# Mamba-2 scan and low-rank mixer: one more block of batch 0 in split one-pass products, and all pieces in another order

## The chip, the cores and the metric

The kernel runs on one core of a Trainium2 chip. The metric is the device time of one execution in microseconds. Before the change it is 234.9 us, the median of three runs (232.25, 234.90, 235.66).

## What is computed

Two blocks follow one another. The first is a Mamba-2 scan over 4 batches, 8 heads, 768 steps, head dimension 32 and state size 16, in chunks:

```python
for c in range(nc):
    cum = np.cumsum(la, axis=-1)
    L = np.exp(cum[..., :, None] - cum[..., None, :]) * causal
    y_intra = ((Cc @ Bc.T) * L) @ xc
    y_inter = (Cc @ state) * np.exp(cum)[..., None]
    y[:, :, sl] = y_intra + y_inter
    state = decay_full * state + (Bx * decay_from_j).sum(axis=2)
```

Its output, regrouped to `x` of shape (4, 768, 256), goes through a mixer, all in fp32:

```python
h = x.transpose(0, 2, 1) @ U @ V          # rank 32, over the sequence
u = x + h.transpose(0, 2, 1)
out = u + np.maximum(u @ w_ch1, 0.0) @ w_ch2     # 256 -> 1024 -> 256
```

The inputs U, V, w_ch1 and w_ch2 arrive as fp64 words and are turned into fp32 on the chip.

## The kernel before

The order of all work is written out by hand, in five strings, `PLANS` (lines 31 to 68). PLANS[0] is the order of the loads on SP's queue; PLANS[1] to [4] are the orders of the pieces. `follow` (line 909) reads a plan word by word and issues the instructions of each; each engine executes its own in that order. Words with a scan letter act on pair k = 3 x (batch) + the word's number, where a pair is 256 steps of the sequence; plan b works on batch b, so `m-1` in plan 1 is pair 2, in batch 0. Words with a mixer letter carry a lag: `U1.0.3` in plan 1 is batch 1 - 1 = 0, block 0, row group 3. A block is 384 tokens, half a sequence.

Scan letters, each with its engine:

| word | what | engine |
|---|---|---|
| P, Q | B and C times decay factors (`prep`, line 436) | VectorE |
| D, E | B times decay to the end (`decayed`, 448) | VectorE; GpSimd in batch 0 |
| T, V | transposes of those (`turning`, 460) | TensorE, then ScalarE, in part VectorE |
| g | products C B (`gram`, 495), into four PSUM banks x, x, z, z | TensorE |
| m, M | causal mask of the x banks, of the z banks (`mask`, 510) | VectorE |
| s, u | chunk states; their decayed sum (`state`, 529, `update`, 545) | TensorE; VectorE |
| i, j, n | the output's parts from the state and from within the chunk (`inter`, `intra`) | TensorE; j may need a small VectorE copy `settled` |
| y, t, O | copy out of PSUM, transpose to token order | ScalarE; TensorE |

The whole program's letters: `A`, `k`, `K` make the decay factors; `c` converts a piece of weights from fp64 words to fp32 in three parts with two ScalarE operations among five VectorE operations (`to_fp32`, 379; c0 is U and V, c1 to c5 are w_ch1, c6 to c9 w_ch2); `R` splits a quarter of a weight in two parts (`refine`, 416; R0 to R3 for w_ch1, R4 to R7 for w_ch2); `v` spreads V; `F n` puts n idle 128-column products into the next PSUM bank (`fill` and `idle`, 130 to 150).

Mixer letters (`mixer`, 692): `p` and `x` are the low-rank products with U and V, `a` adds them to u. Then each block's two large products are made in one of two ways.

- *Plain*, in batch 0 only: `U` (`plain`, 761) makes one 128-row group of relu(u @ w_ch1) in fp32, two products of 128x128 by 128x384; `d` (`down`, 795) makes the second product in four pieces of four products each and then two pieces of transposes and the output copy. It reads the fp32 weights `w1f` and `w2f`.
- *Split*, everywhere else: every fp32 number is written as a near half of 12 bits and a far half; a product is then three products in the type fp32r (near x near, far x both, and so on)[...]. `S` (`split`, 740) splits u: one ScalarE and two VectorE operations. `f` (`first`, 772) makes four of the six products of a row group and has ScalarE rescale the sum, `e` (`second`, 778) the other two and the near half of the relu, `h` (`third`, 786) takes the far half on VectorE and, at every second row group, a third tile that joins both (`joined`, 735). `d` is then twelve pieces of four one-pass products and two of transposes.

The products go to the PSUM tags x and z, two banks each, alternately; x, z are shared with `g` and `x`. Tiles of the tag `words` (15 buffers of 4 KB per partition) hold raw weight words, conversion temporaries, the relu's plain output (four tiles for a block) or its three halves (twelve tiles for a block). The tile for the split u takes the place of `w1f`, so S needs R0 to R3 and all U of w1f to be done.

Of the kernel before, what the change touches and what calls it, by code (L numbers as in the profile page):

```python
# [10 lines left out]
FP32 = mybir.dt.float32  # L11
INT32 = mybir.dt.int32
UINT32 = mybir.dt.uint32
FP32R = mybir.dt.float32r
WCOLS = 512
NWORDS = 15


NEAR = 1.0 - 2.0 ** -13
# [2 lines left out]
ALU = mybir.AluOpType  # L22
# [7 lines left out]

PLANS = {
    0: (
        'V0 B0 X0 B1 X1 B2 X2 B3 U0 w0 w1 X3 w2 B4 X4 w3 w4 w5 B5 w6 X5 w7 B6 w8 X6 '),
    1: (
        'A0 A1 Q-3.0 Q-3.2 Q-3.1 k0 V-3.0.0 V-3.1.1 Q-2.0 K0 F2 g-3 Q-2.2 m-3 M-3 Q-2.1 V-2.0.2 '
        'D-3 F1 s-3 D-2 V-2.1.2 n-3 u-3 Q-1.0 g-2 Q-1.2 i-3 V-1.0.2 m-2 Q-1.1 M-2 F1 V-1.1.3 '
        'E-1.0 F2 s-2 j-3 y-3 g-1 u-2 n-2 E-1.1 i-2 s-1 m-1 j-2 u-1 y-2 M-1 F2 O-3.0 P0 n-1 c0 '
        'i-1 c0 j-1 c0 y-1 t-2 T0 O-1.1 c2 c1 D0 v0 c2 c1 p1 c1 T0 x1 s0 a1.0 c2 a1.1 c3 U1.0.0 '
        'U1.0.1 u0 c3 U1.1.0 D1 U1.1.1 P1 T1 c3 g0 i0 m0 M0 T1 c4 c4 U1.0.2 U1.0.3 s1 c5 c4 c6 c5 '
        'R1 F1 U1.1.2 U1.1.3 u1 n0 L4 g1 P2 D2 j0 T2 T2 c6 m1 U1.0.4 M1 c5 U1.0.5 y0 U1.1.4 c8 '  # L40
        'U1.1.5 c7 i1 c6 c8 c7 R4 n1 g2 P3 j1 s2 m2 u2 y1 L5 R2 M2 R0 U1.0.6 t0 U1.0.7 c7 T3 R3 '
        'T3 U1.1.6 D3 U1.1.7 n2 i2 g3 c9 P4 c8 D4 T4 t1 R6 m3 c9 M3 c9 R2 P5 R1 T4 d1.0 d1.0 d1.0 '
        'R4 j2 s3 R3 D5 y2 u3 d1.0 R7 d1.0 L6 t2 R6 g4 p0 d1.0 m4 M4 R5 R7 n3 '),
    2: (
        'x1 s1 a1.0 d2.1 L4 R0 R5 S1.0 d2.1 D3 d2.1 a1.1 f1.0.0 f1.0.1 u1 T2 T2 P3 e1.0.0 d2.1 '
        'f1.0.2 e1.0.1 f1.0.3 e1.0.2 f1.0.4 e1.0.3 f1.0.5 h1.0.0 h1.0.1 h1.0.2 e1.0.4 h1.0.3 '
        'f1.0.6 e1.0.5 i0 h1.0.4 f1.0.7 e1.0.6 d2.1 e1.0.7 j0 h1.0.5 h1.0.6 d2.1 h1.0.7 y0 T3 T3 '
        'g2 m2 i1 n1 s2 M2 d1.0 d1.0 S1.1 u2 f1.1.0 f1.1.1 d1.0 d1.0 e1.1.0 s3 D4 e1.1.1 P4 '
        'h1.1.0 d1.0 f1.1.2 d1.0 f1.1.3 e1.1.2 h1.1.1 d1.0 d1.0 h1.1.2 j1 d1.0 e1.1.3 y1 u3 '
        'h1.1.3 f1.1.4 t0 d1.0 d1.0 f1.1.5 e1.1.4 d1.0 e1.1.5 L5 f1.1.6 h1.1.4 h1.1.5 f1.1.7 t1 '  # L50
        'e1.1.6 T4 e1.1.7 h1.1.6 h1.1.7 n2 i2 d1.0 g3 T4 d1.0 j2 d1.1 d1.1 d1.1 d1.1 m3 y2 d1.1 '
        'd1.1 M3 P5 d1.1 d1.1 d1.1 d1.1 d1.1 t2 d1.1 p0 D5 g4 d1.1 m4 M4 d1.1 '),
    3: (
        'x1 a1.0 n0 i0 s1 a1.1 j0 S1.0 y0 f1.0.0 f1.0.1 f1.0.2 e1.0.0 e1.0.1 T2 u1 f1.0.3 e1.0.2 '
        'h1.0.0 f1.0.4 h1.0.1 e1.0.3 T2 h1.0.2 h1.0.3 t0 f1.0.5 e1.0.4 f1.0.6 e1.0.5 f1.0.7 '
        'h1.0.4 e1.0.6 i1 e1.0.7 n1 s2 g2 h1.0.5 h1.0.6 j1 h1.0.7 d1.0 m2 d1.0 d1.0 M2 S1.1 y1 '
        'f1.1.0 f1.1.1 d1.0 e1.1.0 e1.1.1 h1.1.0 d1.0 d1.0 f1.1.2 f1.1.3 h1.1.1 u2 d1.0 e1.1.2 '
        'e1.1.3 d1.0 h1.1.2 i2 h1.1.3 d1.0 d1.0 f1.1.4 f1.1.5 n2 e1.1.4 e1.1.5 j2 f1.1.6 h1.1.4 '
        'h1.1.5 y2 f1.1.7 t1 e1.1.6 t2 h1.1.6 e1.1.7 p0 h1.1.7 d1.0 d1.0 '),
    4: (  # L60
        'x1 a1.0 d2.0 d2.0 a1.1 d2.1 d2.1 S1.0 d2.1 d2.1 f1.0.0 d2.1 d2.1 f1.0.1 e1.0.0 d2.1 '
        'e1.0.1 h1.0.0 d2.1 f1.0.2 d2.1 h1.0.1 f1.0.3 d2.1 d2.1 d2.1 e1.0.2 f1.0.4 e1.0.3 f1.0.5 '
        'h1.0.2 f1.0.6 h1.0.3 e1.0.4 h1.0.4 e1.0.5 f1.0.7 d2.1 e1.0.6 h1.0.5 h1.0.6 d2.1 e1.0.7 '
        'h1.0.7 d1.0 S1.1 d1.0 d1.0 d1.0 d1.0 d1.0 d1.0 f1.1.0 f1.1.1 d1.0 e1.1.0 d1.0 e1.1.1 '
        'h1.1.0 d1.0 f1.1.2 h1.1.1 d1.0 d1.0 f1.1.3 e1.1.2 f1.1.4 h1.1.2 e1.1.3 d1.0 f1.1.5 '
        'f1.1.6 e1.1.4 h1.1.3 f1.1.7 e1.1.5 h1.1.4 e1.1.6 h1.1.5 h1.1.6 d1.0 e1.1.7 h1.1.7 d1.1 '
        'd1.1 d1.1 d1.1 d1.1 d1.1 d1.1 d1.1 d1.1 d1.1 d1.1 d1.1 d1.1 d1.1 '),
}


# [1 line left out]
def kernel(  # L72
# [27 lines left out]
    nc = tc.nc  # L100
    P = 128
    NB, NH, S, D = x.shape
# [3 lines left out]
    DM = NH * D  # L106
# [3 lines left out]
    NCB = DM // P  # L110
    HS = S // 2
    W = DF // 4
    NBL = S // HS
    NQ = NM // 2
    Q = 32
# [23 lines left out]
    def bank(tag, *dims):  # L139
        t = psum.tile([P, *dims], FP32, tag=tag, name=tag, bufs=BANKS[tag])  # L140
        if fills[0]:
            idle(t if len(dims) == 1 else t.rearrange(
                {2: "p a b -> p (a b)", 3: "p a b c -> p (a b c)"}[len(dims)]), fills[0])
        fills[0] = 0
        return t

    def fill(n):
# [10 lines left out]
        out=a_sb,  # L158
        in_=a.rearrange("(g b) h (c s) -> g (b h c) s", g=2, s=P).rearrange(
            "g r s -> r g s"))  # L160
# [36 lines left out]
    w1 = [const.tile([P, NCB, DF], FP32R, name=f"w1{i}") for i in range(3)]  # L197
    w1all = mix.tile([P, NQ, NCB, W], FP32, tag="u", name="w1f", bufs=1)
    w1f = [w1all[:, c] for c in range(NQ)]
    w2 = [const.tile([P, NM, DM], FP32R, name=f"w2{i}") for i in range(3)]  # L200
# [56 lines left out]
    ident = const.tile([P, P], FP32)  # L257
# [28 lines left out]
    for v in range(2):  # L286
        half = slice(v * H, v * H + H)
        nc.vector.tensor_tensor(out=ref[half, half], in0=upto[half, half],
                                in1=low[v][half, half], op=ALU.subtract)
# [22 lines left out]
    for b in range(NB):  # L312
        g, o = divmod(b * NH * NC, R)
        nc.vector.tensor_scalar(
            out=la[:, b].rearrange("p c h -> p h c"),
            in0=la_ps[:, g, o:o + NH * NC].rearrange("p (h c) -> p h c", h=NH),
# [10 lines left out]
    for v in range(2):  # L327
        half = slice(v * H, v * H + H)
# [363 lines left out]
    def mixer(b):  # L692
# [34 lines left out]
        def block(n, k):  # L727
            return uT[:, n, ts(k, HS)]
# [19 lines left out]
        def products(t, pairs, start):  # L748
            for lhsT, rhs in pairs:
                nc.tensor.matmul(out=t, lhsT=lhsT, rhs=rhs, start=start, stop=True,  # L750
                                 skip_group_check=True)
                start = False

        def scaled(t):
            nc.scalar.activation(t, t, AF.Copy, scale=1.0 + EPS)  # L755
# [30 lines left out]
        def third(j, m):  # L786
# [5 lines left out]
            if m % 2:  # L792
                joined(near, far, both)

        def down(j):

            def terms(n, which, half):
                return [(w2[v][:, m, ts(n, P)], gs[j, m // 2][v][:, m % 2])
                        for v in which for m in range(NQ * half, NQ * half + NQ)]

            def whole(n, t):
                u = block(n, j)
                nc.vector.tensor_tensor(out=u, in0=t, in1=u, op=ALU.add)  # L803

            ts_ = [bank("xz"[n], HS) for n in range(NCB)] if b else None
            if b:
                for v in range(2):
                    for n in range(NCB):
                        for half in range(2):
                            products(ts_[n], terms(n, (v,), half), v + half == 0)  # L810
                            if v and half:
                                scaled(ts_[n])
                            yield
            for n in range(NCB):
                t = ts_[n] if b else bank("xz"[n], HS)
                for half in range(2):
                    if b:
                        products(t, terms(n, (2,), half), False)
                    else:
                        products(t, [(w2f[m // 2][:, m % 2, ts(n, P)], gT[j, m // 2][:, m % 2])  # L820
                                     for m in range(NQ * half, NQ * half + NQ)], half == 0)
                    if half:
                        whole(n, t)
                    yield
            o = (mix.tile([P, 2 * WCOLS], FP32, tag="o", name="o") if b else raw.tile(
                [P, 2 * WCOLS], FP32, tag="words", name="words", bufs=NWORDS))
            o = o[:, :HS // P * DM].rearrange("p (k n d) -> p k n d", k=HS // P, n=NCB)
            for n in range(NCB):
                t = bank("w", HS // P, P)
                for k in range(HS // P):  # L830
                    nc.tensor.transpose(out=t[:, k], in_=block(n, j)[:, ts(k, P)], identity=ident)  # L831
                nc.scalar.copy(out=o[:, :, n], in_=t)
                if n:
                    nc.sync.dma_start(
                        out=out[b].rearrange("(j k p) m -> j p k m", j=NBL, p=P)[j],
                        in_=o.rearrange("p k n d -> p k (n d)"))
                yield

        us, gs, gT = {}, {}, {}
        downs = {}  # L840

        def piece(j):
            next(downs.setdefault(j, down(j)))

        return SimpleNamespace(p=project, x=mixed, a=added, S=split, f=first, e=second, h=third,
                               d=piece, U=plain)
# [50 lines left out]
    def ytokens_of(k, v):  # L897
# [9 lines left out]
                 v=lambda n: spread())  # L907
# [49 lines left out]
```

## Time and profile before

The profiled execution took 233.18 us, of which the span of the profile is 231.5; the median of the runs is 234.9. TensorE's granted clock was 1.00 throughout.

| row of the profile | count | busy us | mean ns |
|---|---|---|---|
| L750 products, one pass (u and words, x and z) | 576 records | 124.1 | 337 to 347 |
| L750 products, plain, up (yT) | 64 records | 23.6 | 496, 487 |
| L750 products, plain, down (words, o) | 64 records | 21.9 | 489 |
| L789 VectorE, far half of the relu (`third`) | 48 | 26.6 | 554 |
| L737 VectorE, joined halves of the relu | 24 | 23.0 | 958 |
| L755 ScalarE, rescaling | 60 | 28.6 | 476 |
| L135 TensorE, fills (all forms) | 18 records | 6.0 | 275 to 928 |

"Busy" of a matmul includes time in which it overlaps its neighbours in the array, so a mean is longer than the distance from one to the next. Where a count of work is wanted, the distance between starts on the timeline is the better measure. A plain product leaves two records, a one-pass product one.

### The profile page before, as it was taken

The numbers are of one execution on the slowest core, as the hardware profiler recorded it, in microseconds if no ns is written. First come the engines' busy times: TensorE is split into PE (matmuls) and PEld (weight loads), VectorE is DVE, ScalarE is ACT, GpSimd is POOL, SyncE is SP. The second block draws the span as 40 slices with busy tenths as digits, with TensorE's granted clock in tenths as the row PEclk, the third lists the DMA queues.
The fourth block names the chain that finished last, engine by engine and source line by source line (L and its number), as shares of the span: only waits on it lengthen the run. The fifth ranks groups of instructions, "written<-read, shape, count | busy, mean of one in ns | idle before, by whom it ended". The sixth has DMA issues, their size and how long they took to land.

```text
span 231.5 us, 6973 instructions
## 1 busy us (share of the span) xinstructions
PE 222.2 (96%) x3010; PEld 183.0 (79%) x3010; DVE 159.6 (69%) x341; ACT 122.3 (53%) x287; POOL 6.7 (3%) x22
## 2 busy tenths in 40 slices
PE   7988899999999999999999999999999999999992
PEld 4857656566665756889999897988988799999991
DVE  3487799988989879399557517898447635836720
ACT  3243665968946651775555413783635334834711
POOL 4041000000000000000000000000000000000000
PEclk9999999999999999999999999999999999999999
DMA  3994779899940080005300102000000010110101
GB/s 77 128 131 75 187 134 282 176 230 143 121 63 4 3 156 3 3 0 109 56 1 3 69 2 70 4 1 6 0 3 0 21 49 0 35 37 0 36 32 68
DMA packets 69202, 14.56 MB, mean 63 GB/s; under 512 B 63476, under 2 KB 67380, under 8 KB 69172
## 3 DMA queue, kind: packets, MB, share of 16 engines
q1 hardware_dynamic: 69172, 14.13, 31.0%
q8 instruction: 23, 0.38, 0.7%
q14 instruction: 7, 0.06, 0.1%
HBM read 10.98 MB, written 3.15 MB: 61 GB/s over the span
## 4 chain that ended last, share of the span: by engine, by line
PE 94%; DVE 2%; issue 1%; ACT 1%; POOL 0%; POOLq 0%; ACTq 0%
PE x L750 32%; PE z L750 31%; PE y L630 4%; PE y L654 4%; PE x L504 3%; PE w L831 3%; PE w L704 3%; PE w L472 2%; PE w L675 2%; PE w L539 2%; PE x L135 2%; PE x L715 1%; PE z L504 1%; PE z L715 1%; PE x L472 1%
## 5 line engine op out<-in xcount | busy, mean ns | idle before, releaser
L750 PE MATMUL z<-u,w 128*128 128x384 f32 x144 | 33.0, 344 | 0.0
L750 PE MATMUL x<-u,w 128*128 128x384 f32 x144 | 32.9, 347 | 0.0
L755 ACT ACTIVATE x<-x 128x384 f32<-128x384 f32 x30 | 14.3, 476 | 31.0 <-PE x L750 30.4
L750 PE MATMUL x<-words,w 128*128 128x384 f32 x144 | 29.2, 341 | 0.3 <-DVE M L517 0.3
L750 PE MATMUL z<-words,w 128*128 128x384 f32 x144 | 29.0, 337 | 0.0
L750 PEld LDWEIGHTS x<-u,w 128*128 128x128 f32 x144 | 25.1, 188 | 1.1 <-ACT x L755 0.2
L750 PEld LDWEIGHTS x<-words,w 128*128 128x128 f32 x144 | 24.9, 188 | 0.8 <-DVE M L517 0.4
L750 PEld LDWEIGHTS z<-words,w 128*128 128x128 f32 x144 | 25.2, 188 | 0.2 <-issue 0.2
L750 PEld LDWEIGHTS z<-u,w 128*128 128x128 f32 x144 | 24.9, 188 | 0.5
L789 DVE SCALAR_TENSOR_TENSOR words<-x,words 128x384 fp32r<-128x384 f32 x24 | 13.3, 554 | 17.2 <-ACT words L784 17.1
L737 DVE SCALAR_TENSOR_TENSOR words<-words 128x768 fp32r<-128x768 f32 x24 | 23.0, 958 | 1.7 <-PE z L750 0.7
L755 ACT ACTIVATE z<-z 128x384 f32<-128x384 f32 x30 | 14.3, 477 | 10.6 <-PE z L750 10.1
L789 DVE SCALAR_TENSOR_TENSOR words<-z,words 128x384 fp32r<-128x384 f32 x24 | 13.3, 554 | 4.6 <-ACT words L784 4.4
L784 ACT ACTIVATE words<-x 128x384 fp32r<-128x384 f32 x24 | 11.8, 493 | 4.5 <-PE x L750 4.1
L784 ACT ACTIVATE words<-z 128x384 fp32r<-128x384 f32 x24 | 11.9, 494 | 4.0 <-PE z L750 3.9
L630 PE MATMUL y<-T,Sm 32*64 32x64 f32 x352 | 12.8, 239 | 0.5 <-DVE settled L581 0.3
L803 DVE TENSOR_TENSOR yT<-x,yT 128x384 f32<-128x384 f32 x8 | 4.4, 554 | 12.6 <-PE x L750 12.6
L630 PEld LDWEIGHTS y<-T,Sm 32*64 32x64 f32 x352 | 9.6, 131 | 4.1 <-issue 0.7
L559 DVE SCALAR_TENSOR_TENSOR S<-S,kept,w 128x64 f32<-128x64 f32 x40 | 11.2, 280 | 2.1 <-PE w L539 0.5
L750 PE MATMUL x<-yT,w1f 128*128 128x384 f32 x32 | 11.9, 496 | 0.0
L445 DVE TENSOR_TENSOR BC<-bc,F 128x512 f32<-128x512 f32 (+2 forms) x18 | 9.9, 557 | 2.8 <-DMA bc<-in_B_dram 2.6
L750 PE MATMUL z<-yT,w1f 128*128 128x384 f32 x32 | 11.7, 487 | 0.0
(152 smaller groups left out, 386.8 us busy)
## 6 DMA issues: line engine op xcount, KB each, us to landing
words<-in_moe_w_ch_dram SPq DMA_DIRECT2D x7, 512.0 KB, 4.9
x<-in_x_dram SPq DMA_DIRECT2D x24, 128.0 KB, 3.4
out_dram<-o SPq DMA_DIRECT2D x6, 384.0 KB, 2.5
bc<-in_B_dram SPq DMA_DIRECT2D x24, 64.0 KB, 3.6
bc<-in_C_dram SPq DMA_DIRECT2D x12, 128.0 KB, 3.7
out_dram<-words SPq DMA_DIRECT2D x2, 384.0 KB, 3.5
words<-in_moe_w_ch_dram SPq DMA_DIRECT2D x2, 256.0 KB, 3.8
words<-in_moe_V_dram SPq DMA_DIRECT2D x1, 192.0 KB
```

What stands on the lines that cost most here:

```text
L445: nc.vector.tensor_tensor(out=part, in0=bc_sb[k].rearrange("p h i c n -> p (i c) h n")[:, g], in1=F[:, b, q].rearrange("p h i c -> p (i c) ...
L472: nc.tensor.transpose(out=tp[:, i, v], in_=s["BC"][:, i, c + v].rearrange("p h n -> p (h n)"), identity=ident)
L504: nc.tensor.matmul(out=g[r][cols, c], lhsT=s["T"][rows, 0, c, cols], rhs=s["Cm"][rows, :, :, ts(2 * c + p, Q)].rearrange("r v t i -> r v i ...
L559: done = nc.vector.scalar_tensor_tensor(out=new, in0=st["S", b], scalar=kept[:, b, j, None], in1=add, op0=ALU.mult, op1=ALU.add)
L630: product = nc.tensor.matmul(out=y[p][ts(r % 2, H), r // 2, c], lhsT=own[ts(r, Q)], rhs=s["T"][ts(r, Q), 1, :, ts(2 * c + p, Q)].rearrange ...
L654: product = nc.tensor.matmul(out=y[p][ts(i, Q), n, c], lhsT=x_sb[k][half, c, h], rhs=s["M"][half, h // 2, c, h % 2], start=fresh(k, p, [i] ...
L704: nc.tensor.matmul(out=p[ts(q, Q)], lhsT=U_sb[:, c], rhs=ytok[b][:, c, ts(q // 2, P)], start=(c == 0), stop=(c == NC - 1), skip_group_chec ...
L737: nc.vector.scalar_tensor_tensor(out=both, in0=near.bitcast(FP32), scalar=-EPS, in1=far.bitcast(FP32), op0=ALU.mult, op1=ALU.add)
L750: nc.tensor.matmul(out=t, lhsT=lhsT, rhs=rhs, start=start, stop=True, skip_group_check=True)
L755: nc.scalar.activation(t, t, AF.Copy, scale=1.0 + EPS)
L784: nc.scalar.activation(gs[j, m // 2][0][:, m % 2], t, AF.Relu, scale=NEAR)
L789: nc.vector.scalar_tensor_tensor(out=far[:, m % 2], in0=gs["t", j, m], scalar=0.0, in1=near[:, m % 2].bitcast(FP32), op0=ALU.max, op1=ALU. ...
```

## The change

The constant `PLAIN` becomes 1: in batch 0 only block 0 is still made with plain products. Block 1 gets the split form, so its eight `U1.1` words go, and `S1.1`, `f1.1.0` to `7`, `e1.1.0` to `7` and `h1.1.0` to `7` come in plan 1 (the last as `h2.1.7` in plan 2), with fourteen pieces `d2.1` instead of six in plan 2. In all plans the order of the words is another; plan 1 starts its conversions `c` earlier, has 26 fill units where all plans together had 9, and its first mixing word x1 comes after more of batch 1's scan. In the loads, X3 and B4 now stand ahead of w0 to w2, and w5 to w7 ahead of X5, with B5 earlier. The new function `rows` is used only if `b >= ROWS`, with ROWS = 9, so for no batch.

```diff
+PLAIN = 1
+ROWS = 9
...
     0: (
-        'V0 B0 X0 B1 X1 B2 X2 B3 U0 w0 w1 X3 w2 B4 X4 w3 w4 w5 B5 w6 X5 w7 B6 w8 X6 '),
+        'V0 B0 X0 B1 X1 B2 X2 B3 U0 X3 B4 w0 w1 w2 X4 w3 w4 B5 w5 w6 w7 X5 w8 B6 X6 '),
     1: (
-        'A0 A1 Q-3.0 Q-3.2 Q-3.1 k0 V-3.0.0 V-3.1.1 Q-2.0 K0 F2 g-3 Q-2.2 m-3 M-3 Q-2.1 V-2.0.2 '
-        'D-3 F1 s-3 D-2 V-2.1.2 n-3 u-3 Q-1.0 g-2 Q-1.2 i-3 V-1.0.2 m-2 Q-1.1 M-2 F1 V-1.1.3 '
-        'E-1.0 F2 s-2 j-3 y-3 g-1 u-2 n-2 E-1.1 i-2 s-1 m-1 j-2 u-1 y-2 M-1 F2 O-3.0 P0 n-1 c0 '
-        'i-1 c0 j-1 c0 y-1 t-2 T0 O-1.1 c2 c1 D0 v0 c2 c1 p1 c1 T0 x1 s0 a1.0 c2 a1.1 c3 U1.0.0 '
-        'U1.0.1 u0 c3 U1.1.0 D1 U1.1.1 P1 T1 c3 g0 i0 m0 M0 T1 c4 c4 U1.0.2 U1.0.3 s1 c5 c4 c6 c5 '
-        'R1 F1 U1.1.2 U1.1.3 u1 n0 L4 g1 P2 D2 j0 T2 T2 c6 m1 U1.0.4 M1 c5 U1.0.5 y0 U1.1.4 c8 '
-        'U1.1.5 c7 i1 c6 c8 c7 R4 n1 g2 P3 j1 s2 m2 u2 y1 L5 R2 M2 R0 U1.0.6 t0 U1.0.7 c7 T3 R3 '
-        'T3 U1.1.6 D3 U1.1.7 n2 i2 g3 c9 P4 c8 D4 T4 t1 R6 m3 c9 M3 c9 R2 P5 R1 T4 d1.0 d1.0 d1.0 '
-        'R4 j2 s3 R3 D5 y2 u3 d1.0 R7 d1.0 L6 t2 R6 g4 p0 d1.0 m4 M4 R5 R7 n3 '),
+        'K0 D-3 A0 Q-3.0 F5 A1 Q-3.2 Q-3.1 V-3.0.0 V-3.1.1 Q-2.0 Q-2.2 k0 g-3 m-3 M-3 V-2.0.2 F1 '
+        's-3 Q-2.1 V-2.1.2 n-3 D-2 Q-1.0 u-3 s-2 F2 g-2 Q-1.2 u-2 i-3 Q-1.1 E-1.0 E-1.1 m-2 '
+        'V-1.0.2 M-2 V-1.1.3 g-1 j-3 P0 T0 m-1 y-3 M-1 T0 c0 s-1 F2 g0 c0 i-2 D0 c0 u-1 n-2 j-2 '
+        'P1 y-2 T1 T1 m0 c1 M0 F3 s0 D1 c1 u0 c2 c1 c3 i-1 c2 F3 O-3.0 n-1 F2 t-2 j-1 s1 c2 c3 c3 '
+        'y-1 v0 u1 R1 F4 O-1.1 c5 c4 n0 R0 i0 g1 R1 m1 p1 M1 j0 P2 x1 c5 a1.0 y0 a1.1 c6 c6 T2 T2 '
+        'c4 c5 U1.0.0 c6 U1.0.1 L4 D2 U1.0.2 U1.0.3 n1 c4 i1 t0 g2 s2 j1 R4 m2 c7 y1 M2 c8 c8 c7 '
+        'P3 L5 R3 U1.0.4 U1.0.5 u2 c7 F1 U1.0.6 T3 T3 U1.0.7 R5 n2 g3 R3 D3 i2 P4 R2 m3 T4 M3 c8 '
+        'T4 F3 t1 g4 j2 s3 m4 c9 c9 y2 c9 R2 M4 R0 D4 d1.0 d1.0 d1.0 P5 L6 S1.1 R4 R6 d1.0 f1.1.0 '
+        'f1.1.1 R5 f1.1.2 e1.1.0 f1.1.3 e1.1.1 u3 e1.1.2 d1.0 e1.1.3 h1.1.0 h1.1.1 f1.1.4 h1.1.2 '
+        't2 d1.0 f1.1.5 R7 f1.1.6 f1.1.7 h1.1.3 e1.1.4 e1.1.5 R6 h1.1.4 e1.1.6 e1.1.7 h1.1.5 p0 '
+        'T5 T5 h1.1.6 i3 '),
...
-            ts_ = [bank("xz"[n], HS) for n in range(NCB)] if b else None
-            if b:
+            parts = b or j >= PLAIN
+            ts_ = [bank("xz"[n], HS) for n in range(NCB)] if parts else None
+            if parts:
...
-                t = ts_[n] if b else bank("xz"[n], HS)
+                t = ts_[n] if parts else bank("xz"[n], HS)
...
-                    if b:
+                    if parts:
                         products(t, terms(n, (2,), half), False)
```

Plans 2 to 4 are other orders of the same words as before, except for the words of batch 0's block 1 named above; one `n`, `i`, `M` or `h` word here and there stands in the neighbouring plan.

## The prediction

> **What bounds the kernel now.** I read the page's busy shares and slices first, then busy times by stage, then the engines' timelines around the place where the change acts.
>
> ```profile
> span 231.5 us, 6973 instructions
> PE 222.2 (96%) x3010; PEld 183.0 (79%) x3010; DVE 159.6 (69%) x341; ACT 122.3 (53%) x287; POOL 6.7 (3%) x22
> PE   7988899999999999999999999999999999999992
> DVE  3487799988989879399557517898447635836720
> PE 94%; DVE 2%; issue 1%; ACT 1%; POOL 0%; POOLq 0%; ACTq 0%
> ```
>
> TensorE is the chain: 94% of the path. But in slices 5 to 18 (from about 29 us) VectorE is nearly as full as TensorE. The windows, cut at events of the TensorE timeline, say how full:
>
> ```profile
> 4.40:20.00 15.60, 13.79 (x246) 11.33 (x252) 9.57 (x30) 5.68 (x22) 2.53 (x4) 1.00 0.94 131
> 20.00:31.20 11.20, 10.49 (x375) 7.91 (x374) 8.80 (x30) 6.80 (x19) 1.48 (x3) 1.00 0.62 142
> 31.20:65.80 34.60, 34.31 (x579) 22.07 (x580) 31.77 (x77) 25.73 (x58) 0.00 (x0) 1.00 0.91 175
> 65.80:81.40 15.60, 15.60 (x236) 10.02 (x234) 14.18 (x29) 9.43 (x21) 0.00 (x0) 1.00 0.07 12
> 81.40:141.90 60.50, 60.29 (x730) 51.18 (x722) 39.19 (x75) 29.20 (x69) 0.00 (x0) 1.00 0.20 39
> ```
>
> The columns after the length are PE, PEld, DVE, ACT, POOL busy. 31.2 us is where batch 0's mixing product `x1` starts; 65.8 is where its first down product `d1.0` starts (I call this **the mark**); 81.4 ends plan 1. From 4.4 to 65.8 VectorE is busy 9.57 + 8.80 + 31.77 = 50.1 of 61.4 us, so idle 11.3: 6.0 before 20 us, 2.4 up to 31.2, 2.8 after. After 81.4 it is busy 65%, with room. Two lines of timelines show that both engines arrive at the mark together:
>
> ```profile
> 65.01 0.76 DVE L517 TENSOR_TENSOR M<-x,causal 128x256 int32<-128x256 int32 x2 [0.58 <-PE z L504]
> 65.78 5.33 PE L750 MATMUL x<-words,o 128*128 128x384 f32 x16
> ```
>
> The mask `m3` frees the two x banks at 65.7; the down product, which writes an x bank, starts at 65.78. The stretch is balanced: work taken from TensorE there buys nothing unless VectorE comes sooner too.
>
> [...]the eight plain products from 65.78 to 70.94 take 5.16 us, 0.645 each (two records a product), and eight one-pass products take 0.174 each:
>
> ```profile
> 131.48 1.55 PE L750 MATMUL z<-words,w 128*128 128x384 f32 x8
> 132.87 1.55 PE L750 MATMUL x<-words,w 128*128 128x384 f32 x8
> ```
>
> (1.39 us from start to start, over 8). The ratio is 3.7. [...] PE counts 10.49 of 11.2 us busy between 20 and 31.2, yet the pieces there, by start to start, hold less. So I count work by start-to-start times.
>
> **The change part by part.**
>
> *TensorE, products.* 32 plain products go (16 up, 16 down), 96 one-pass products come: 32 x 0.645 = 20.6 us out, 96 x 0.174 = 16.7 in, **-3.9 us**.
>
> *TensorE, fills.* The plans before hold 9 fill units, the new ones 26. A 128-column unit takes 0.27 (two at 19.39, next work at 19.93). Twelve new ones of that size are 3.2; five of 48 columns I put at 0.1 each (unmeasured; 0.05 to 0.27): **+3.7**. TensorE's total is then unchanged within 0.2. Fills lie where TensorE would wait; they cost only if the wait is not there.
>
> *VectorE.* One more split (L732 954 + L737 958 ns), eight `third` (L789, 554 each), four joins (958 each): 1.9 + 4.4 + 3.8 = +10.2; three settle copies of 0.152 go: **+9.7**. *ScalarE:* ten more scalings of 0.476 and a near half of 0.855: **+5.6**, in a queue 53% busy; the split's near half stands on the path to the first one-pass product, but at a point where TensorE still has plain products.
>
> *Behind the mark.* Of the pieces ahead of the mark, the new order takes away the eight `U1.1` (16 plain products, 10.3) and adds g4 (0.63), s3 (0.38), j2 (0.43) and the 17 fill units (3.7): TensorE has 10.3 - 1.4 - 3.7 = 5.2 less ahead. As its total is 0.2 less, **5.0 us more lies behind the mark.** Before, 231.5 - 65.8 = 165.7 us follow it. If that stretch runs as densely as now, the end is mark + 170.7: break-even is a mark at 60.8.
>
> *When is the mark reached?* TensorE alone could be there at 60.6. VectorE could not. In the new order the x banks go to g4, so the mark needs `m4`. Ahead of m4 VectorE has all that it had ahead of m3, plus R1 and R3 (1.33 each, as from 68.86 to 70.19), M3 and m4 (0.67 each, as from 65.01 to 65.68) and j2's copy (0.12), less the first part of c9 (0.67, as from 60.79 to 61.46) and D4 (0.34): **+3.1**. With the same idle time that is 65.7 + 3.1 = 68.8. But conversions `c` now start before the first batch's scan is through, in VectorE's idle places: of the 5.2 us idle after 20 us I expect 4.4 to be filled, the first 6.0 to stay (they are input arrival and the decay chain). The 4.4 is from walking the new order by hand with the rows' durations, which leaves 6.9 of idle. On the way x1 comes near 42 instead of 31.2: it needs the banks that M1 frees, and ahead of M1 stand the 18.4 us of before plus c3 (2.5), the rest of c2 (1.1), the starts of c4 and c5 (1.3), R1 (1.3), two masks (2.7), u0 and u1 (2.4), P1 and P2 (1.2), D1 (0.3), 31.2 in all, after 4.4 and 6 to 7 of idle. So the mark is at 68.8 - 4.4 = **64.4**.
>
> *Moved, at nothing.* x1 comes 11 us later: nothing but `a` and `U` waits for it, and the DVE work ahead of it is work that the mark needs anyway. On SP's queue X3 and B4 now pass w0 to w2, and four down-weight loads pass B5 and X5; w0 and w2 still wait for m-1 and M-1, which I place at 22 to 24 us as now. They land in 4 to 5 us by the issue table, and c1 is due at 28, c3 at 32: covered by other VectorE work. If that cover goes, c3 is late next. GpSimd has the same 22 instructions. The twelve buffers for block 1's halves come after the four of block 0 are free (its last plain product precedes e1.1.0), out of 15: no wait.
>
> *After the mark.* VectorE gets S1.1, h1.1 and R4 to R7 in a stretch with 22.1 us of TensorE work against 20.6 of VectorE. Bounds: 0 if it keeps pace, +1.2 if x1 of batch 1 waits for the last join; I take 0, because plans 2 to 4 take 146.1 us (81.4 to 227.5) for pieces that sum to 138.8, an excess that may also shrink.
>
> *Sum:* 64.4 + 170.7 = 235.1 in place of 231.5: **+3.6 us** (1.6%). The profiled execution took 233.18 with 1.7 around the span, 1.7 below the median of the runs, 234.9. I add 3.6 to the median: **238.5**.
>
> **The rivals.** A change of 2% is about what a measurement of this kernel can tell from none.
>
> *R0, likeliest (0.52): VectorE sets the mark between 62.5 and 65.5,* end +1.7 to +4.7: 236.6 to 239.6.
>
> *R1 (0.38), slower: the idle places are not filled.* VectorE runs its queue in order. Each conversion has three parts with two ScalarE operations between them, and in the stretch 13 to 42 us they stand between masks, updates and settle copies for which TensorE is waiting: an early `c` that waits for ScalarE or a weight load blocks those. The price is one us per us of idle kept: with none filled the mark is at 68.8 and the end at 239.5, time 242.9. It decides from a mark at 65.5 (less than 3.3 filled), where the loss passes 4.7. For it: VectorE is idle for 8% of 31.2 to 65.8 even where its queue always holds a conversion. Against it: the only conversion that waits for ScalarE in the dense stretch does so for 0.5 us (L402 at 67.5).
>
> *R2 (0.10), the saving gets through.* VectorE's early idle shrinks by 3 us or more, K0 and D-3 being first now, and later stages, with one-pass pieces to interleave, recover some. The mark is at 60 to 62.5: end between 230.7 and 233.2, or, with fills that only replace waits and nothing late at all, 231.5 - 3.9 = 227.6; time 231.0 to 236.6. Even its end is -1.7%, so a gain over 2% needs a second saving that I cannot name: 0.05 in all.
>
> That the change would not do what it says is excluded: the instruction lists hold 704 products at that line against 640.
>
> **How the numbers follow.** 238.5 is R0's value. Low 232.0 holds most of R2; high 243.5 takes in R1's full price. Faster 0.05 (tail of R2), same 0.57 (R0 and the rest of R2), slower 0.38 (R1).
>
> **What would show it.** x1 near 42 and the mark near 64 on TensorE's timeline; VectorE over 93% busy from 21 us to the mark; plain product records down from 128 to 64 and one-pass ones up from 576 to 672; PE waits on VectorE masks in the first 60 us. Wrong if the mark comes before 61, if VectorE has over 2 us of idle between 42 us and the mark, or if the time behind the mark differs from 170.7 by more than 2.

## The result, and the profile after

The changed kernel takes 245.12 us (median of four runs, 243.62 to 247.20) where the kernel before takes 234.11 in the same comparison: a ratio of 1.048 [1.036, 1.060]. It is slower by nearly 5%, above the predicted 232.0 to 243.5. The profiled execution took 247.20 us with a span of 245.5, 2.1 above the median; the predicted span was 235.1. Executions over 1.5% longer than the shortest of their kernel are left out of every ratio below, which leaves `e3_split_old` and `e6_fill2` without one, and the traces of these two and of `e3b_split_old` are of such executions, so that a few us in them need not come from the edit.

First the page of the changed kernel: its busy shares, slices of 6.1 us, and the shares of the chain that ended last.

```profile
span 245.5 us, 7105 instructions
PE 228.3 (93%) x3060; PEld 196.6 (80%) x3060; DVE 167.2 (68%) x352; ACT 127.0 (52%) x298; POOL 6.4 (3%) x22
PE   7997669769999999999999998999999999999993
DVE  3246675969899999976776887459735864574731
PEclk9999577997999999999999999999999999999999
PE 84%; DVE 4%; ACT 3%; issue 3%; SPq 2%; DMA 1%; POOL 0%; DVEq 0%; POOLq 0%; ACTq 0%
```

Three things differ from before (slices are counted from 0). VectorE's row is no longer full from slice 5 on; the dense part begins at slice 9. TensorE, 94% of the chain before, is 84%, and the lost tenth went to many small owners. And the granted clock, for which the page of the kernel before has no dip, is at 0.5 to 0.7 in slices 4 to 6 and again at 0.7 in slice 9.

All of that lies ahead of the mark. These two rows, of the instructions of one source line, give x1 and the mark by their first start ("54.1 to", "77.2 to"):

```profile
L720 PE MATMUL x<-V,pT x16: 481/585/842, 54.1 to 196.0; 32*128 32x384 f32 x16
...
L755 PE MATMUL x<-words,o x16: 486/486/590, 77.2 to 82.1; 128*128 128x384 f32 x16
```

x1 starts at 54.1 (forecast 42, before 31.2), the mark at 77.2 (forecast 64.4, before 65.8), and 245.5 - 77.2 = 168.3 us follow (forecast 170.7, before 165.7). So the mark is 12.8 us later than forecast, the rest 2.4 shorter: together the 10.4 us by which the span was missed. From x1 to the mark it is 23.1 us, close to the forecast 22.4. The miss is ahead of x1.

The windows of the changed kernel, cut at 20 and 31.2 us as for the kernel before, at x1 and at the mark (columns as before: length, then PE, PEld, DVE, ACT, POOL busy, clock, DMA share, GB/s):

```profile
4.40:20.00 15.60, 14.45 (x200) 12.53 (x200) 6.27 (x23) 4.97 (x19) 1.24 (x2) 1.00 0.99 141
20.00:31.20 11.20, 7.77 (x155) 5.63 (x155) 6.99 (x22) 4.27 (x12) 2.06 (x4) 0.67 0.48 86
31.20:54.10 22.90, 17.89 (x502) 13.17 (x502) 17.36 (x49) 12.95 (x31) 0.51 (x1) 0.87 0.91 218
54.10:77.20 23.10, 22.72 (x409) 14.72 (x408) 20.57 (x44) 16.12 (x35) 0.00 (x0) 0.93 0.54 74
77.20:245.50 168.30, 162.50 (x1798) 149.09 (x1798) 113.78 (x204) 86.95 (x200) 0.00 (x0) 1.00 0.11 27
```

VectorE is busy 6.27 + 6.99 + 17.36 + 20.57 = 51.2 us of the 72.8 up to the mark, so idle 21.6, against a forecast of 6.9: 9.3 before 20 us, 9.7 between 20 us and x1, 2.5 after. Its work is what I had counted (53.1), 1.9 less even; 14.7 us more of idle less 1.9 of work is the 12.8. Between 20 and 54 us no engine is full. What delays whom there is seen in pieces. TensorE's timeline of the changed kernel at the start (start, duration, line, operation, count):

```profile
7.21 2.35 PE L140 MATMUL w<-ident 128*128 128x48 f32 x10
9.49 0.64 PE L347 MATMUL w<-la,ref 128*64 128x24 f32 x8
10.06 0.48 PE L477 MATMUL w<-ident,BC 128*128 128x128 f32 x1
10.91 0.95 PE L477 MATMUL w<-ident,BC 128*128 128x128 f32 x3 [0.38 <-DVE BC L450]
```

The five narrow fills of `F5`, ten records, occupy TensorE from 7.21 to 9.49: 2.3 us, 0.46 each. Most of the decay factors stand behind them, and with them all but VectorE's first `prep`. The first gram product g-3 starts at 15.76 instead of 12.48.

These 0.46 us are a price at half rate, by the equal products shown below; the clock rows hide it. The clock record of these two traces begins late, and the rows count all time ahead of it as 1.00. It begins, with full rate, at 16.9 us in the changed kernel and at 10.3 in the kernel before. Five equal products of the decay factors (48 or 40 columns, two records each) show what came earlier. The kernel before, just behind its 10.3 us (first and last of the five, and the start of the next group):

```profile
10.83 0.32 PE L357 MATMUL z<-la,after 128*128 128x48 f32 x2
...
11.65 0.39 PE L367 MATMUL z<-la,low 128*128 128x40 f32 x2
11.87 0.68 PE L135 MATMUL x<-ident 128*128 128x256 f32 x2
```

and the changed kernel, ahead of its 16.9:

```profile
4.24 0.63 PE L362 MATMUL z<-la,after 128*128 128x48 f32 x2
...
5.93 0.63 PE L372 MATMUL z<-la,low 128*128 128x40 f32 x2
6.36 1.03 PE L352 MATMUL w<-la,ref 128*128 128x24 f32 x4
```

From start to start it is 1.04 us for the five, 0.21 each, in the first and 2.12 us, 0.42 each, in the second. The ratio is 2.0, hence "half rate". So "1.00 throughout", as I had written of the kernel before, holds from 10.3 us on, and the 1.00 of the first window above is no full rate.

The masks m-1 and M-1 then start at 27.41 and 28.08 instead of 21.66 and 24.32, and the first load of w_ch1, which is held for a mask, starts late with them (the waits of the load queue, by line: total, times, longest):

```profile
SPq L244 <- DVE M L522: 6.3, 1, 6.3
```

The first conversion, `c0`, stands behind both masks in VectorE's queue. VectorE's timeline of the changed kernel:

```profile
27.41 0.75 DVE L522 TENSOR_TENSOR M<-x,causal 128x256 int32<-128x256 int32 x2 [1.05 <-PE z L509]
28.08 0.74 DVE L522 TENSOR_TENSOR M<-z,causal 128x256 int32<-128x256 int32 x2
28.74 0.35 DVE L397 TENSOR_SCALAR words<-words 128x384 int32<-128x384 int32 x1
```

and of the kernel before:

```profile
21.66 0.75 DVE L517 TENSOR_TENSOR M<-x,causal 128x256 int32<-128x256 int32 x2
...
24.32 0.75 DVE L517 TENSOR_TENSOR M<-z,causal 128x256 int32<-128x256 int32 x2
...
25.58 0.35 DVE L392 TENSOR_SCALAR words<-words 128x384 int32<-128x384 int32 x1
```

So the conversions, which were to start earlier, start 3.2 us later than before. TensorE's waits of the changed kernel, over the whole span:

```profile
PE x L720 <- ACT words L401: 1.9, 1, 1.9
PE y L635 <- issue: 1.7, 1, 1.7
PE x L140 <- POOL ident masks.py:199: 1.4, 1, 1.4
PE w L544 <- issue: 1.3, 1, 1.3
PE w L544 <- ACT Cm L487: 1.1, 1, 1.1
```

No wait is longer than 1.9 us; there is no one culprit. The rows put down to "issue" are new at this size. In TensorE's timeline of the changed kernel they stand in the middle of a group of equal matmuls whose operands are all there:

```profile
21.71 0.33 PE L544 MATMUL w<-x,bd 64*32 64x64 f32 x11 [1.27 <-issue]
...
36.78 0.41 PE L635 MATMUL y<-T,Sm 32*64 32x64 f32 x9 [1.67 <-issue]
```

The clock falls in the same stretch. Windows of 4 us, changed kernel:

```profile
20.00:24.00 4.00, 2.47 (x79) 1.70 (x79) 2.07 (x8) 0.08 (x1) 1.30 (x3) 0.96 0.81 106
24.00:28.00 4.00, 3.21 (x50) 2.56 (x51) 2.73 (x9) 1.42 (x5) 0.75 (x3) 0.50 0.02 3
28.00:32.00 4.00, 2.90 (x38) 1.51 (x38) 2.94 (x9) 2.77 (x7) 0.00 (x0) 0.50 0.65 170
```

and the kernel before in the first of them:

```profile
20.00:24.00 4.00, 4.00 (x198) 3.31 (x198) 2.69 (x11) 1.22 (x5) 0.97 (x2) 1.00 0.18 49
```

Where TensorE was busy without a break before, it now works 2.47 of 4 us, and in the next windows runs at half clock. An estimate of the price from the windows above: busy time times the missing clock, 7.77 x 0.33 + 17.89 x 0.13 + 22.72 x 0.07 = 6.5 us of TensorE time. The half rate from 10.3 to 16.9 us, in which TensorE is busy 6.2 us, adds 3.1. Not all of this is on the path.

### The profile page after: what moved, and what is told of

Read it like the earlier page. It is cut to its first block, busy times and chain, and to the rows that moved or that the text cites. A ratio compares the mean times of both kernels' runs of the same rounds, so it can differ in the third digit from the quotient of the medians.

```text
span 245.5 us, 7105 instructions
## 1 busy us (share of the span) xinstructions
PE 228.3 (93%) x3060; PEld 196.6 (80%) x3060; DVE 167.2 (68%) x352; ACT 127.0 (52%) x298; POOL 6.4 (3%) x22
## 4 chain that ended last, share of the span: by engine, by line
PE 84%; DVE 4%; ACT 3%; issue 3%; SPq 2%; DMA 1%; POOL 0%; DVEq 0%; POOLq 0%; ACTq 0%
PE x L755 28%; PE z L755 27%; PE y L635 3%; PE y L659 3%; PE w L477 3%; PE x L509 2%; PE x L140 2%; PE w L544 2%; PE w L864 2%; PE w L709 2%; SPq L221 2%; PE w L140 1%; PE x L720 1%; DMA bc<-in_B_dram 1%; PE w L680 1%
## 5 line engine op out<-in xcount | busy, mean ns | idle before, releaser
L755 PE MATMUL x<-u,w 128*128 128x384 f32 x168 | 38.5, 344 | 0.0
L755 PE MATMUL z<-u,w 128*128 128x384 f32 x168 | 38.0, 341 | 0.0
L755 PE MATMUL x<-words,w 128*128 128x384 f32 x168 | 34.1, 340 | 0.4 <-DVE yT L729 0.4
L755 PE MATMUL z<-words,w 128*128 128x384 f32 x168 | 34.3, 336 | 0.0
L760 ACT ACTIVATE x<-x 128x384 f32<-128x384 f32 x35 | 16.9, 482 | 31.5 <-PE x L755 30.8
L755 PEld LDWEIGHTS x<-u,w 128*128 128x128 f32 x168 | 29.4, 188 | 0.5
L755 PEld LDWEIGHTS z<-u,w 128*128 128x128 f32 x168 | 29.4, 188 | 0.3
L755 PEld LDWEIGHTS z<-words,w 128*128 128x128 f32 x168 | 29.6, 188 | 0.0
L794 DVE SCALAR_TENSOR_TENSOR words<-x,words 128x384 fp32r<-128x384 f32 x28 | 15.5, 554 | 15.4 <-ACT words L789 15.4
L835 DVE TENSOR_TENSOR yT<-x,yT 128x384 f32<-128x384 f32 x8 | 4.5, 557 | 17.0 <-PE x L755 17.0
L509 PE MATMUL x<-Cm,T 32*64 32x128 f32 x192 | 11.6, 336 | 1.1 <-DVE settled L586 0.8
L659 PEld LDWEIGHTS y<-M,x 64*32 64x32 f32 x768 | 8.8, 107 | 3.9 <-issue 3.6
L659 PE MATMUL y<-M,x 64*32 64x64 f32 x768 | 11.0, 228 | 0.9 <-issue 0.9
```

The lines of the kernel that those rows point to most:

```text
L509: nc.tensor.matmul(out=g[r][cols, c], lhsT=s["T"][rows, 0, c, cols], rhs=s["Cm"][rows, :, :, ts(2 * c + p, Q)].rearrange("r v t i -> r v i ...
L659: product = nc.tensor.matmul(out=y[p][ts(i, Q), n, c], lhsT=x_sb[k][half, c, h], rhs=s["M"][half, h // 2, c, h % 2], start=fresh(k, p, [i] ...
L794: nc.vector.scalar_tensor_tensor(out=far[:, m % 2], in0=gs["t", j, m], scalar=0.0, in1=near[:, m % 2].bitcast(FP32), op0=ALU.max, op1=ALU. ...
```

## The experiments

The theories after the result: the loss comes from the order ahead of x1 (a late start, fills, a longer chain of dependent pieces), from the traffic of the loads moved ahead, or from the split itself. Each kernel below was timed in rounds with the kernel before. It is the changed kernel but for the edit shown; only the words of the plans that differ are shown.

| run | median us, all runs | ratio to before | x1 | mark | after the mark | VectorE busy / idle, 4.4 us to mark | half rate there (full rate first at) |
|---|---|---|---|---|---|---|---|
| before | 234.1 | 1 | 31.2 | 65.8 | 165.7 | 50.1 / 11.3 | 5.9 (10.3) |
| after | 245.1 | 1.048 [1.036, 1.060] | 54.1 | 77.2 | 168.3 | 51.2 / 21.6 | 29.5 (16.9) |
| e1_loads | 250.1 | 1.059 [1.048, 1.070] | 57.2 | 78.9 | 168.3 | 51.1 / 23.4 | 31.2 (15.1) |
| e2_start | 242.6 | 1.035 [1.027, 1.043] | 50.4 | 72.4 | 168.6 | 51.8 / 16.2 | 18.7 (9.5) |
| e4_plain_new | 254.0 | 1.085 [1.076, 1.093] | 54.0 | 76.0 | 176.6 | 51.3 / 20.3 | 32.3 (16.2) |
| e5_nofill | 242.4 | 1.036 [1.029, 1.043] | 49.5 | 71.2 | 169.6 | 51.7 / 15.1 | 30.5 (14.5) |
| e6_fill2 | 248.4 | none | 57.5 | 79.6 | 167.9 | 51.6 / 23.6 | 25.6 (23.2) |
| e8_start_nofill | 242.9 | 1.039 [1.030, 1.047] | 50.6 | 72.4 | 169.9 | 51.3 / 16.7 | 34.9 (18.8) |
| e9_old_to_x1 | 241.3 | 1.025 [1.013, 1.036] | 31.4 | 68.4 | 172.1 | 52.3 / 11.7 | 16.7 (10.9) |
| e3b_split_old | 247.0 | 1.053 [1.044, 1.062] | 35.0 | 68.1 | 179.7 | 49.9 / 13.8 | 26.2 (25.6) |

All columns from x1 on are of one profiled execution each. The last gives the us at half rate between 4.4 us and the mark, the time ahead of the clock record counted as half, and in brackets when the record begins. The trace of `after` is its longest execution, 2.1 us above the median, so a mark that is set against its 77.2 can look up to some 2 us better than it is.

**e1_loads: the loads of before.**

```diff
-        'V0 B0 X0 B1 X1 B2 X2 B3 U0 X3 B4 w0 w1 w2 X4 w3 w4 B5 w5 w6 w7 X5 w8 B6 X6 '),
+        'V0 B0 X0 B1 X1 B2 X2 B3 U0 w0 w1 X3 w2 B4 X4 w3 w4 w5 B5 w6 X5 w7 B6 w8 X6 '),
```

> The changed kernel with the load order of before (w0 to w2 ahead of X3 and B4 again). Theory A, traffic: in the changed kernel the transfers of X3 and B4 run at 18 to 24 us, and TensorE's gap of 1.27 us inside s-2 at 20.4 and the half clock after it follow from that; then the gap is under 0.7, the clock stays at 1.0 to 30 us, x1 comes 3 to 6 us sooner and the time is 239 to 242 us. Theory B, order of the pieces: the gaps come from the pieces' own waits; the time stays within 2 us of 245.

It came out no faster, above both theories; that it is slower than the changed kernel is not clear, as the two intervals overlap. Half of theory A came true all the same. The break of 1.27 us inside s-2 is gone, and the half clock begins at 28.8 us instead of 23.7. But TensorE now waits for VectorE's products with a B that arrives late and that the new order wants earlier (TensorE's waits of `e1_loads`):

```profile
PE w L477 <- DVE BC L450: 5.0, 2, 4.6
```

The new order of the loads has its price, and it belongs to the new order of the pieces: undone alone, it opens a wait in another place.

**e2_start: the start of before, up to g-3, fills included.**

```diff
-        'K0 D-3 A0 Q-3.0 F5 A1 Q-3.2 Q-3.1 V-3.0.0 V-3.1.1 Q-2.0 Q-2.2 k0 g-3 m-3 M-3 V-2.0.2 F1 '
+        'A0 A1 Q-3.0 Q-3.2 Q-3.1 k0 V-3.0.0 V-3.1.1 Q-2.0 K0 F2 g-3 Q-2.2 m-3 M-3 D-3 V-2.0.2 F1 '
```

> The changed kernel with the start of before up to the first gram g-3 (A0 and A1 first, K0 last, no F5). Theory A, start: K0 and five narrow fills ahead of A1 put the factors F, and with them g-3, 3.2 us later (15.7 against 12.5); undone, g-3 is at 12.5 again and everything follows: 241 to 242 us, less if the clock stays up too. Theory B: the delay is absorbed by later waits, 244 to 246 us.

g-3 starts at 12.27, 3.5 us earlier than in the changed kernel, and the mark is at 72.4, 4.8 us earlier; the medians are 2.6 us apart, just short of theory A, and the intervals of the ratios overlap. So the late start does not seem to be absorbed in this order. How much of the gain is the order and how much the full rate, which comes at 9.5 us here and at 16.9 in the changed kernel, this run does not separate.

**e3_split_old and e3b_split_old: the split alone, in the order of before.** Loads and plan 1 of before up to the mark, without `U1.1`; then the words of the changed tail.

```diff
-        ... c3 U1.0.0 U1.0.1 u0 c3 U1.1.0 D1 U1.1.1 P1 T1 c3 g0 ... c9 M3 c9 R2 P5 R1 T4 d1.0 d1.0 d1.0
+        ... c3 U1.0.0 U1.0.1 u0 c3 D1 P1 T1 c3 g0 ... c9 M3 T4 c9 d1.0 d1.0 d1.0 R2 P5 R1 R3 j2 s3
```

> The split of block 1 kept, but loads and plan 1 up to the first plain down product in the order of before, with the U1.1 words left out; after it the changed order. Theory A, order: the loss is the new order of the first 54 us; the mark comes at 63 to 68 us, and the time is 234 to 240 us (the saving of 3.9 us is not seen, because VectorE sets the mark). Theory B, split: the extra VectorE work of 9.7 us is what costs; 241 us or more.

The first version (254.8 us) had a flaw of my own: T4 stood behind R2 and R1 while TensorE waited for it (6.2 us at the states, L544), so its mark, 74.4, tells little. In the second T4 stands ahead of them:

> As e3_split_old, with the flaw of that order mended: in e3 the last transposes T4 stood behind R2 and R1, so their ScalarE copy waited for those, and s3, ahead of the mark, waited 6.2 us for it. Here T4 stands ahead of them and s3 behind the first plain products. Theory A: the split alone, in the order of before, is bound by VectorE's conversions ahead of the mark, which then comes at 65 to 69 us although TensorE has 10 us less to do there; the time is 236 to 243 us, no faster than before. Theory B, that the split saves its 3.9 us once the order is that of before: mark at 56 to 61, time 229 to 233 us.

The mark is at 68.1, as theory A had it (the time, 247.0, is above its 243). x1, ahead of which all words and loads are those of before, comes at 35.0 instead of 31.2, as full rate comes at 25.6 us in this execution; from x1 to the mark it takes 33.1 us instead of 34.6, although TensorE has 10.3 us less to do there. The windows of `e3b_split_old` from 36 to 68 us and after:

```profile
36.00:68.00 32.00, 25.64 (x538) 17.02 (x539) 30.95 (x76) 21.61 (x49) 0.00 (x0) 0.92 0.96 182
68.00:247.00 179.00, 168.52 (x1880) 153.43 (x1878) 116.24 (x207) 90.56 (x207) 0.00 (x0) 0.98 0.12 27
```

VectorE is busy 30.95 of 32 us where TensorE is 25.64: here VectorE sets the mark, as the prediction said of this stretch. Behind the mark this kernel takes 11.4 us more than the changed one. A wait of 4.4 us of a gram product for VectorE's sum of the down products (L835), at the joint of two orders, is part of it; the rest was not followed up, so its end says nothing of the split.

**e4_plain_new: the new order, block 1 plain again.** Plan 1 has a `U1.1` at each `f1.1`, and no S, e and h; plan 2 has six `d2.1`.

```diff
-PLAIN = 1
+PLAIN = 2
...
-        'T4 F3 t1 g4 j2 s3 m4 c9 c9 y2 c9 R2 M4 R0 D4 d1.0 d1.0 d1.0 P5 L6 S1.1 R4 R6 d1.0 f1.1.0 '
-        'f1.1.1 R5 f1.1.2 e1.1.0 f1.1.3 e1.1.1 u3 e1.1.2 d1.0 e1.1.3 h1.1.0 h1.1.1 f1.1.4 h1.1.2 '
+        'T4 F3 t1 g4 j2 s3 m4 c9 c9 y2 c9 R2 M4 R0 D4 d1.0 d1.0 d1.0 P5 L6 R4 R6 d1.0 U1.1.0 '
+        'U1.1.1 R5 U1.1.2 U1.1.3 u3 d1.0 U1.1.4 '
```

> The new order, but block 1 of batch 0 in plain products again (U1.1 words where f1.1 stood, no S1.1, e1.1, h1.1, six pieces d2.1). Theory A, order: x1 at 54 and the mark at 77 us as in the changed kernel, and TensorE's 3.9 us of plain work more behind it: 246 to 250 us. Theory B, split: 233 to 238 us.

The mark hardly moves (76.0), and the time behind it grows by 8.3 us; the time, 254.0, is above both theories. So the new order is late without the split, and within that order, which was made for it, the split is a gain of about 8 us.

**e5_nofill and e6_fill2: no fills in plan 1, and twice as many.** In plan 1 alone; every `F` word goes, or has its number doubled.

```diff
-        'V-1.0.2 M-2 V-1.1.3 g-1 j-3 P0 T0 m-1 y-3 M-1 T0 c0 s-1 F2 g0 c0 i-2 D0 c0 u-1 n-2 j-2 '
+        'V-1.0.2 M-2 V-1.1.3 g-1 j-3 P0 T0 m-1 y-3 M-1 T0 c0 s-1 g0 c0 i-2 D0 c0 u-1 n-2 j-2 '
```

> The changed kernel without any of its 26 fill units in plan 1. Theory A, fills hold the clock: without them TensorE is busy less in 15 to 40 us, the half clock lasts as long or longer, and the time is 245 to 250 us. Theory B, fills are on the path: F5 alone took 2.2 us ahead of the factors; without fills the time is 240 to 243 us.

> The changed kernel with every fill doubled (52 units). Theory A, fills hold the clock: the half clock in 24 to 41 us gets shorter and the time falls to 240 to 244 us. Theory B, fills are on the path: 248 to 252 us.

Without fills the mark comes 6.0 us earlier and the median is 2.8 lower, as theory B had it, although the first dip of the clock lasts 17.1 us instead of 10.2. The clock row of `e5_nofill`:

```profile
PEclk9997558799999999999999999999999999999999
```

The fills stand in TensorE's queue ahead of work that is due, and here they cost more than they give, though the two intervals overlap. What twice as many do is not shown. The trace of `e6_fill2`, with its mark at 79.6, is of its longest execution, 249.22 us; its shortest, 244.24, lies within the changed kernel's own 243.62 to 247.20. Nor is it shown that fills hold the clock up. With none, 26 and 52 units TensorE was at half rate for 30.5, 29.5 and 25.6 us up to the mark, in one execution each, and executions of one and the same order differ by more than that (`before` and `e3b_split_old` up to x1: 10.3 and 25.6 us).

**e8_start_nofill: both edits that helped.** The plan of `e2_start` without any `F`.

```diff
-        'A0 A1 Q-3.0 Q-3.2 Q-3.1 k0 V-3.0.0 V-3.1.1 Q-2.0 K0 F2 g-3 Q-2.2 m-3 M-3 D-3 V-2.0.2 F1 '
+        'A0 A1 Q-3.0 Q-3.2 Q-3.1 k0 V-3.0.0 V-3.1.1 Q-2.0 K0 g-3 Q-2.2 m-3 M-3 D-3 V-2.0.2 '
```

> The changed kernel with both edits that helped alone: the start up to the first gram product in the order of before (which moved the first plain down product from 77.2 to 72.4 us) and no fill units at all in batch 0 (77.2 to 71.2). Theory A (they are two separate costs on the path, which add): first plain down product at 66 to 69 us, time behind it 168 to 170, in all 235 to 239 us. Theory B (both act through the same few us, the delay ahead of the first gram product, and the rest is the clock, which stays at half speed longer without fills): first plain down product at 70 to 72 us, 239 to 242 us.

The two do not add: the mark is at 72.4 again. In this execution full rate first comes at 18.8 us, where it came at 9.5 in `e2_start`, and the time from 20 us to x1 stays loose (windows of `e8_start_nofill`):

```profile
20.00:32.00 12.00, 9.55 (x244) 7.41 (x227) 9.35 (x29) 4.83 (x13) 1.84 (x4) 0.59 0.84 170
32.00:50.60 18.60, 12.69 (x358) 9.16 (x356) 13.74 (x38) 10.55 (x26) 0.00 (x0) 0.71 0.93 221
```

and the breaks put down to "issue" grew. TensorE's waits of `e8_start_nofill` from 20 to 50 us:

```profile
PE y L635 <- issue: 3.4, 1, 3.4
PE w L544 <- issue: 1.7, 1, 1.7
```

What is won at one place is partly lost at the next. This is nearer to theory B, though both its numbers are just missed (72.4 for 70 to 72, and a median of 242.9 for 239 to 242).

**e9_old_to_x1: the order ahead of x1 undone.** Loads and plan 1 of before up to x1 and a few words behind it, then all words that are left in the order of the change.

```diff
-        'K0 D-3 A0 Q-3.0 F5 A1 Q-3.2 Q-3.1 V-3.0.0 ... g1 R1 m1 p1 M1 j0 P2 x1 c5 a1.0 y0 a1.1 '
+        'A0 A1 Q-3.0 Q-3.2 Q-3.1 k0 V-3.0.0 ... D0 v0 c2 c1 p1 c1 T0 x1 s0 a1.0 c2 a1.1 c3 U1.0.0 '
+        'U1.0.1 u0 c3 D1 P1 T1 c3 g0 T1 m0 M0 s1 u1 R1 c5 c4 n0 R0 i0 g1 R1 m1 M1 j0 P2 c5 y0 '
```

> Only the order ahead of x1 is undone: the pieces and loads of before up to x1 and the four words behind it, then everything that is left in the order of the change, with the second block split. Theory A (the whole loss lies in the order ahead of x1, and the tail of the change is worth keeping): x1 at 31 to 33 us, the first plain down product at 64 to 68 us, time behind it 168 to 170 us, in all 233 to 238 us, no slower than before. Theory B (the products of batch 0 that no longer stand ahead of x1 are missed behind it, where VectorE is already full): x1 at 31 to 33, the first plain down product at 70 us or later, 239 us or more.

x1 is at 31.4 and the mark at 68.4, 8.8 us earlier than in the changed kernel and 0.4 outside what theory A allowed; the time, 241.3, is on the side of theory B. The windows of `e9_old_to_x1` up to x1, to the mark, and behind it:

```profile
20.00:31.40 11.40, 10.67 (x380) 8.02 (x378) 8.99 (x31) 6.96 (x19) 1.48 (x3) 1.00 0.69 154
31.40:68.40 37.00, 29.53 (x628) 19.31 (x628) 33.97 (x79) 25.96 (x56) 0.00 (x0) 0.86 0.87 166
68.40:240.50 172.10, 164.86 (x1803) 151.43 (x1798) 113.81 (x204) 86.98 (x200) 0.00 (x0) 0.99 0.11 26
```

Up to x1 both the density and the clock of before are back; VectorE's idle time up to the mark is 11.7 us, as before the change (11.3). Behind the mark it takes 3.8 us longer than the changed kernel. Of these a break of 1.9 us at 113.5 on the chain and a dip of the clock right behind it, in the slice from 114 to 120 us, are seen; the rest is open. It is the fastest but one in its mark and the fastest in time of all kernels with the split, and still 1.3 to 3.6% slower than the kernel before; whether by more than 2% is not settled. No version that beats the kernel before came out.

## Why the prediction was wrong, point by point

**Right: the counts, and nearly the time behind the mark.** The one-pass records are 672 and the plain ones 64, as forecast. Behind the mark the six kernels that keep the changed order there and the split (`after`, `e1`, `e2`, `e5`, `e6`, `e8`) take 167.9 to 169.9 us; the forecast 170.7 is 0.8 to 2.8 above. By its own bound of 2 us the prediction is just missed by the changed kernel (168.3), by 0.4, in the direction that it had left open (an excess in plans 2 to 4 that may shrink).

**Right: VectorE's work.** I forecast 53.1 us of it up to the mark. The kernels of the table have 49.9 to 52.3, whatever their order: the mark is 4.4 plus some 50 to 52 plus VectorE's idle time, in every one of them.

**Wrong: the idle time.** The step that failed is "I expect 4.4 to be filled, the first 6.0 to stay", from a walk of the new order by hand. It became 21.6. R1, whose worst case was that none of it is filled, had the right sign, and its mark of 68.8 is near what two kernels with the order of before up to x1 gave, `e3b_split_old` (68.1) and `e9_old_to_x1` (68.4); but it took the old idle time of 11.3 for the upper end. Nothing bounds idle time by what it was in another order. The parts, as far as the runs separate them:

- *The start.* I had counted K0 and D-3 first in favour (R2), and `F5` at 0.1 each. The fills took 0.46 each, 2.3 us in place of 0.5, in front of nearly everything. The price could have been read: products of that width took 0.21 us at full rate in the kernel before, which is twice what I put, and half rate doubled it again. With the start undone the mark gains 4.8 us in the traces (2.6 in the medians).
- *The fills.* "They cost only if the wait is not there" was right as a condition; I then took the wait to be there. Their removal gains 6.0 us in the traces (2.8 in the medians). This includes the start's `F5`, so it overlaps the point above; both edits together gain 4.8.
- *The chain of dependent pieces between g-3 and x1.* I placed m-1 and M-1 "at 22 to 24 us as now"; they came at 27.4 and 28.1, so the weights and `c` came late too. With the order ahead of x1 undone, 8.8 of the 12.8 us are gone. This is the largest part, and it contains the two above and a share of the next.
- *The clock.* The sum took it to be as in the profile before, without saying so. Up to the mark TensorE was at half rate for 29.5 us, before for 5.9. No run restores the clock and nothing else, but two show its price. `e3_split_old` and `e3b_split_old` have the loads and, up to x1, the words of before; full rate comes 11.9 and 15.4 us later in them, and x1 2.4 and 3.8 us later, 0.20 and 0.25 us for each us at half rate. Ahead of x1 the changed kernel is at half rate for 20.3 us more than the kernel before. By that price, which is from another order, an estimate is 4 to 5 of the 12.8 us; it is not separated from the idle time that goes with it.

"Moved, at nothing: x1 comes 11 us later" was wrong by 12 us in its number (54.1 for near 42) and not in what it says of the path: x1 22.9 us later than before is the sign of the lost time, while x1 to the mark took 23.1 us for a forecast 22.4. The remaining 4.0 us between `e9_old_to_x1` (68.4) and the forecast (64.4) are VectorE's places that no conversion filled (11.7 idle for 6.9), less the 0.8 by which its work was smaller.

**What the split is worth** is seen by `e4_plain_new` alone: 8.3 us behind the mark, in an order made for it. The order made to fit it costs 12.8 us more than I forecast, and 11.4 more than the order before, ahead of it.

## What to carry to other kernels

Before an order of dependent pieces is moved, the work that it adds between them can be summed, but its idle time can't: walk the chain from the first product to the first load that waits for it, and let the upper bound of idle time be open. Fill work in a queue that runs in order is free only where the measured wait stands (here the mark came 6.0 us earlier without it), and its price depends on the clock at that place: a 48-column fill took 0.46 us at half rate, and products of that width took 0.21 at full rate in the kernel before. Where one engine was always busy, check what it does to the clock when the new order opens gaps in it: in the changed kernel the clock fell to 0.50 behind 3.41 us in which TensorE was busy 0.62 of the time. And before a clock of 1.00 is believed, set equal products of early and late stretches side by side.

## What the runs showed of the hardware

**The clock and the busy share.** In the changed kernel the clock fell to 0.50 at 23.7 us; the longest single gap of TensorE between 4.4 us and there was 1.27 us. In the eleven traces of this case every stretch between two changes of the clock is a whole multiple of 3.41 us (in the changed kernel, from 16.9 us on: 2, 3, 1, 1, 4, 1 and 55 times that). I cut the full-rate time of each trace into pieces of that length, on the beat of its changes, and took TensorE's busy share in each. All 16 pieces with a share of 0.52 or less were followed by half rate; of 14 pieces from 0.53 to 0.68, six were; of 640 above 0.68, none. In `before` and `after`, with 127 of the pieces, the lowest shares are 0.00 twice (the last piece of each trace), 0.44, 0.45 and 0.62, all followed by half rate, and 0.57, which was not; the rest are 0.74 or more. In the piece ahead of the changed kernel's first dip the share was 0.62, and the one break of 1.27 us makes 0.37 of the 0.38 that are missing.

**When full rate first comes.** In the kernel before it came at 10.3 us, with TensorE busy 8.00 of the 8.00 us from 2 to 10. In `e9_old_to_x1`, `e3_split_old` and `e3b_split_old`, which have the same loads and words up to x1, it came at 10.9, 22.2 and 25.6 us. So the order alone does not set it; what does is open.

**Breaks behind instruction packets.** The breaks put down to "issue" stand after matmul records 219, 473 and 727 in the changed kernel and after 220 and 474 in the kernel before: 254 records apart in both, whatever instruction stands there. They took 0.43 to 0.70 us before, 0.48 to 1.67 in the changed kernel (a later one, after record 2253, took 0.43), and up to 3.43 in `e8_start_nofill`, where the DMA share during the break was 0.79. The profile's page lists a queue of 24 instruction packets with 0.39 MB, some 16 KB each. Their times in the traces fit: all 28 such breaks of 0.4 us or more, in the eleven kernels, end 1.26 to 1.78 us after one of these packets has landed. In the changed kernel that packet started at 19.24 us and TensorE went on at 21.71. In `e1_loads`, whose instructions for TensorE are the same and whose loads alone differ, the packet started at 16.64, and there is no break at that record. That TensorE waits there for its next instructions, and that the order of the loads bears on when they come, is what I infer from these times; no view names such a wait, and why a packet comes late was not tested.

**Plain against one-pass.** From start to start plain products took 0.645 us each and one-pass ones 0.174, while a one-pass record lasts 0.34 (337 to 347 ns in the kernel before), so that records overlap. By the first two, taking block 1 back to plain should cost 3.9 us of TensorE time. `e4_plain_new` showed 8.3 behind the mark, so 4.4 us of it are not product time. Of these, 3.1 are idle time of TensorE, 8.9 us behind the mark for 5.8 in the changed kernel, with one wait of 1.7 us for VectorE's far half of the relu; the rest is open.
